# The last gate's sums: from DVE in the attention heads to POOL and ScalarE in the first units of the token mixing

## The chip, the cores and the metric

The kernel runs on one core of a Trainium2 chip. The metric is the device time of one execution in microseconds (us), as a median of several runs. Five engines work side by side, each in the order of its own instruction list: PE (TensorE, matrix products; its weight loads are listed as PEld), DVE (VectorE), ACT (ScalarE), POOL (GpSimd) and SP (SyncE), which here issues all transfers (DMA). Engines wait for each other by semaphores.

## The reference, cut to what matters

One block on x of 2048 tokens by 1024 channels: a conditioned attention with a memory, then an MLP over the token axis. Six vectors of 1024 come from a conditioning vector `c`; the last one, `gb`, scales the MLP's output.

```python
mod = (_silu(c) @ w_mod).reshape(c.shape[0], 6, 1, -1)
sa, ca, ga, sb, cb, gb = (mod[:, 0], mod[:, 1], mod[:, 2], mod[:, 3], mod[:, 4], mod[:, 5])
h = _layernorm(x, axis=-1) * (1 + ca) + sa
x = x + ga * _A_ref(h, A_wq, A_wk, A_wv, A_wo, A_beta)
h = _layernorm(x, axis=-1) * (1 + cb) + sb
x = x + gb * _B_ref(h, B_w1, B_b1, B_w2, B_b2)
...
# in _B_ref
u = jnp.einsum("bsd,sf->bdf", h, w1) + b1
u = _gelu(u)
y = jnp.einsum("bdf,fs->bds", u, w2) + b2
```

## The kernel before

The work has four stages.

*Start (0 to about 100 us).* `c` passes through SiLU into `sc` (a column) and `scb` (the same 1024 numbers on every partition). The first two vectors, `sa` and `ca`, are made here.

*Heads (to about 990 us).* 32 iterations of four heads each: `project` (matmuls of L194 and L202), `maxima`, `scores`, `values`. A hand-written plan (`plan`, `later`, `todo`) puts side work at given heads n. The remaining four vectors of `mod` are side work: at head 40 + 2j, `mod_fetch(j)` loads 128 rows of `w_mod` transposed (512 KB, tile `rawm`), and two heads later `mod_late(j)` (L531) multiplies them with `scb` on DVE and adds up each row into column j of `mcol`. Eight columns make one vector, so j = 24 to 31 is the gate `gb`. After j = 7 and after j = 31 `mod_rows` transposes the finished columns on PE and writes them to DRAM (`modd`); `spread(dst, i)` (L567) loads row i of `modd` onto all partitions.

*Output projection (to about 1212 us)* of 16 token tiles, with the second layernorm. It ends in the inputs of the mixing.

*Mixing (to the end).* Both products of the MLP use seven products in place of eight (a Strassen scheme, `NPR = 7`). The first half has 28 units: `ph` 0 and 1, `g` 0 to 13. A unit is one `mix`: seven products q of 12 matmuls each. For each unit `prepare` loads 1 MB of weights (`wr`, two buffers), makes the seven operands' sums on DVE, and splits each operand (tile `sp`, seven buffers) into a high part by ACT (L121) and a low part by DVE (L124). A product lands in a PSUM bank and is evicted to `cc`: by ACT (L831) if it is the first to reach its quarter in `ph` 0, otherwise by DVE as an addition (L833). Products 0, 2, 4 and 6 go on in the same bank, so each must be evicted before the next begins. `pcd[g]` keeps the result of `ph` 0. Beside units 1 to 9 of `ph` 0 run the `bias_rows` (L875 to L880): for each of 16 token tiles a row block `x1d` is loaded, `gb * b2` is added by DVE (L879), and the result goes to `x1e`. They need `gb`, which is loaded at the end of unit 1. In `ph` 1 `gb` also multiplies each unit's output (L962). The second half (w2) has 40 units and begins at about 1765 us.

The order of instructions on each engine is fixed when the kernel is compiled: a scheduler takes the program's order as priority and simulates the engines. Tiles with the same tag share their buffers in turn, and a load into a buffer waits for its last reader.

Of the kernel before, what the change touches and what calls it, by code (L numbers as in the profile page):

```python
# [7 lines left out]
F32 = mybir.dt.float32  # L8
# [3 lines left out]
AF = mybir.ActivationFunctionType  # L12
ALU = mybir.AluOpType
# [4 lines left out]
S, D, H, DH, F = 2048, 1024, 32, 32, 3584  # L18
P = 128
# [3 lines left out]
NT = S // P  # L23
# [15 lines left out]
WO0 = 65  # L39
# [6 lines left out]
def attention_and_mlp(ctx, tc, x, wq, wkv, wo, beta, w1, b1, w2, b2, c, wm_a, wm_b, out):  # L46
    nc = tc.nc
    V, A, G, T, SY = nc.vector, nc.scalar, nc.gpsimd, nc.tensor, nc.sync

    dram = ctx.enter_context(tc.tile_pool(name="dram", bufs=1, space=DRAM))  # L50
    oT = dram.tile([NG, P, S], F32, name="oT")
    modd = dram.tile([4, D], F32, name="modd")
    x1d = dram.tile([NT, P, D], F32, name="x1d")
    x1e = dram.tile([NT, P, D], F32, name="x1e")
    hcd = dram.tile([8, P, 7, 512], F32, name="hcd")
# [10 lines left out]
    a = par.__enter__()  # L66
    scb, gaw = (a.tile([P, D], F32, name=n) for n in ("scb", "gaw"))
# [8 lines left out]
    def bank(tag, bufs, name):  # L76
        return psum.tile([P, 512], F32, tag=tag, bufs=bufs, name=name)
# [94 lines left out]
    def keep_w(g):  # L172
        for kind, n in (("v", 4), ("q", 2)):
            for i in range(n):
                SY.dma_start(wsp[g, i if kind == "v" else 4 + i], W[0, g][kind, i].bitcast(F32))
# [126 lines left out]
    b = late.__enter__()  # L302
# [220 lines left out]
    mcol = const.tile([P, 4 * NK], F32, name="mcol")  # L523

    def mod_fetch(j):
        r = a.tile([P, D], F32, tag="raw", bufs=3, name=f"rawm{j}")
        SY.dma_start(r, wm_b[P * j:P * j + P])
        return r

    def mod_late(j, r):  # L530
        V.scalar_tensor_tensor(r, r, 1.0, scb, op0=ALU.mult, op1=ALU.mult, accum_out=mcol[:, j:j + 1])  # L531
        if j == 7:
            mod_rows(0, 8)
        if j == 31:
            V.tensor_scalar_add(mcol[:, 16:24], mcol[:, 16:24], 1.0)
            mod_rows(8, 32)

    def mod_rows(lo, hi):
        n = hi - lo
        ps = bank("ms", 1, f"mlt{lo}")  # L540
        T.transpose(ps[0:n, 0:128], mcol[:, lo:hi], ident)
        row = pj.tile([n, P], F32, tag="tmp", bufs=2, name=f"mrow{lo}")
        A.copy(row, ps[0:n, 0:128])
        SY.dma_start(modd.rearrange("a (b n) -> (a b) n", n=P)[lo:hi], row)
# [3 lines left out]
    def plan(n, f, engines=""):  # L548
        todo.setdefault(n, []).append((f, engines))
# [16 lines left out]
    def spread(dst, i):  # L566
        SY.dma_start(dst, bass.AP(tensor=modd.tensor, offset=modd.offset + D * i, ap=[[0, P], [1, D]]))  # L567
# [19 lines left out]
    def wo_fetch(i):  # L587
        nh, c2 = i // 4, 2 * (i % 4)
        r = a.tile([P, 2, 512], F32, tag="raw", bufs=3, name=f"wor{i}")
        SY.dma_start(r, wo[P * c2:P * c2 + 2 * P, 512 * nh:512 * nh + 512].rearrange("(c p) n -> p c n", p=P))  # L590
        return r

    def wo_split(i, r):

        nh, c2 = i // 4, 2 * (i % 4)
        hi = a.tile([P, 2, 512], F32, tag="raw", bufs=3, name=f"woh{i}")
        for j in range(2):
            G.tensor_tensor(r[:, j], r[:, j], gaw[:, 512 * nh:512 * nh + 512], op=ALU.mult)
            A.copy(hi[:, j].bitcast(F32R), r[:, j])
            V.tensor_tensor(r[:, j].bitcast(F32R), r[:, j], hi[:, j], op=ALU.subtract)  # L600
        for part, t in enumerate((hi, r)):
            SY.dma_start(wos[c2:c2 + 2, nh, :, part].rearrange("c p n -> p c n"), t)

    def later(n, fetch, m, f, engines):

        got = []
        plan(n, lambda: got.append(fetch()))
        plan(m, lambda: f(got[0]), engines)
# [4 lines left out]
    for g in range(2, NG):  # L613
        n = 8 * g - 13
# [2 lines left out]
            later(n + n0, lambda g=g, kind=kind, part=part: fetch_part(g, kind, part),  # L617
                  n + n1, lambda r, g=g, kind=kind, part=part: split_part(g, kind, part, r), "A")
        plan(n + 4, lambda g=g: keep_w(g))
    for j in range(32):  # L620
        n = ML0 + MLS * j
        later(n, lambda j=j: mod_fetch(j), n + 2, lambda r, j=j: mod_late(j, r), "V")
    plan(WO0 - 3, lambda: spread(gaw, 0))
    for i in range(8):
        n = WO0 + WOS * i
        later(n, lambda i=i: wo_fetch(i), n + 2, lambda r, i=i: wo_split(i, r), "G")

    for n in range(-LEADS, 4 * NI + VL):
# [15 lines left out]
        if 4 * NI - 5 <= m < 4 * NI + 3:  # L644
            i = m - 4 * NI + 5
# [46 lines left out]
    def b_tile(pool, nk, q, name):  # L692
        return pool.tile([P, nk, 2, 512], F32R, tag=f"B{q}", bufs=1, name=f"{name}_{q}")
# [144 lines left out]
    def load_b(stg, src, nk, dsts, q, name, bufs=2):  # L838

        r = stg.tile([P, nk, 512], F32, tag="bst", bufs=bufs, name=f"bst{name}_{q}")  # L840
        SY.dma_start(r, src[:, :, SLOT[q]].rearrange("k p n -> p k n"))
        for k in range(nk):
            split(dsts[k], r[:, k], A, V)
# [5 lines left out]
    def y_tile(name):  # L849
        return yb.tile([P, 4, 512], F32, tag="ac", bufs=4, name=name)  # L850
# [31 lines left out]
    def cc_tile(ph, g):  # L882
        cc = cp.tile([P, 4, 512], F32, tag="cc", bufs=3, name=f"cc{ph}_{g}")
        if ph:
            SY.dma_start(cc, pcd[g])
        return cc

    def w2_unit(ph, g):
        k0, nk = sum(KP[:ph]), KP[ph]
        return prepare(w2[g, :, 512 * k0:512 * (k0 + nk)].rearrange("p (b n) -> p b n", b=4), nk)  # L890

    acc = {}

    def start_acc(g, pool):
# [7 lines left out]
    row = 0  # L902
    for u, (ph, g) in enumerate(units):
        cc = cc_next
        if g == 0:
            nxt = {}
        last = u + 1 == len(units)
        if last:
            unit_2 = w2_unit(0, 0)

        def after(q):
            if u < 2:
                n = 7 * u + q
                if n in (2, 5, 8):
                    rest[(2, 5, 8).index(n)]()
            if q == 3 and not last:
                cc_next_[0] = cc_tile(*units[u + 1])
            if g < NG1 - 1:
                return
            if ph == 0:  # L920
                if q % 2 == 0 and q < 6:
                    return
                for r in (q - 1, q) if q < 6 else (q,):
                    if r % 2 == 0:
                        b2_ = y_tile(f"bB1_{r}")
                    a_, b_ = b_tile(b3, 3, r, "bA1"), b2_[:, 2 * (r % 2):2 * (r % 2) + 2].bitcast(F32R)
                    load_b(tp, hcd[4:8], 4, [a_[:, 0], a_[:, 1], a_[:, 2], b_], r, "h4")
                    nxt[r] = (a_, b_)
            else:
                if q in (1, 3, 5, 6):  # L930
                    start_acc({1: 0, 3: 1, 5: 2, 6: 3}[q], yb)
                for i in {3: (0,), 4: (1,), 5: (2, 3), 6: (4, 5, 6)}.get(q, ()):
                    unit_2[1].pop(0)()
                nxt[q] = next_b(tp, 0, q)

        cc_next_ = [None]
        mix(unit, 4, lambda q, k: bA[q][:, k] if k < 3 else bB[q], cc, ph == 0, after)
        cc_next = cc_next_[0]
        if not last:
            unit = prepare(w1[units[u + 1]], 4)  # L940
        if u == 1:
            cw_pool.__exit__(None, None, None)
            tp_pool = tc.tile_pool(name="g1t", bufs=1, reuse_waits="tile")
            tp = tp_pool.__enter__()
            gb = tp.tile([P, D], F32, name="gb")
            spread(gb, 3)
            b1s = tp.tile([P, FT], F32, name="b1s")
            SY.dma_start(b1s, b1)
            b2s = tp.tile([P, NT], F32, name="b2s")
            SY.dma_start(b2s, b2)  # L950
        if ph == 0:
            SY.dma_start(pcd[g], cc)
            if g == NG1 - 1:
                bA, bB = [nxt[q][0] for q in range(NPR)], [nxt[q][1] for q in range(NPR)]
            for tt in range(row, min(row + (0, 1, 2)[min(g, 2)], NT)):
                bias_rows(tt)
                row = tt + 1
            continue
        for m in range(2):
            c2 = cc[:, 2 * m:2 * m + 2].rearrange("p a n -> p (a n)")  # L960
            A.activation(c2, c2, AF.Gelu_apprx_tanh, bias=b1s[:, g + NG1 * m:g + NG1 * m + 1])
            V.tensor_tensor(c2, c2, gb, op=ALU.mult)  # L962
        t = tp.tile([P, 3, 512], F32, tag="tu", bufs=1, name=f"tu{g}")
        t_combos(G, cc[:, 0], cc[:, 1], cc[:, 2], cc[:, 3], t)
        SY.dma_start(ucd[g, :, 0:4], cc)
        SY.dma_start(ucd[g, :, 4:7], t)
# [3 lines left out]
    yac, tp = (ctx.enter_context(tc.tile_pool(name=n, bufs=1, reuse_waits="tile")) for n in ("yac", "g2t"))  # L970
# [59 lines left out]
```

## Time and profile before

| | us |
|---|---|
| median of 3 runs | 2292.65 (2292.54 to 2294.87) |
| the profiled execution | 2297.73 |
| its span, first to last instruction | 2296.0 |
| PE busy | 2223.2 (97%) |
| DVE busy | 1673.7 (73%) |
| ACT busy | 1148.6 (50%) |
| POOL busy | 734.0 (32%) |

All times within the kernel come from the one profiled execution and count from its first instruction. Busy time is the union of an engine's instructions; matmuls overlap each other, so a busy PE is not necessarily PE at its peak. "Idle before" in a row of the timeline is the time that the engine stood still ahead of that instruction, and the name behind the arrow is what ended it. L12 is line 12 of the kernel.

### The profile page before, as it was taken

How to read it: one execution, taken by the hardware profiler on the slowest of the kernel's cores; microseconds unless marked ns; L12 is line 12 of the kernel's file. 1: busy time of each engine (PE TensorE's matmuls, PEld its weight loads, DVE VectorE, ACT ScalarE, POOL GpSimd, SP SyncE). 2: the span in 40 equal slices, each digit the busy share in tenths (PEclk: the TensorE clock that was granted, in tenths of full speed). 3: DMA queues.
4: the chain of work that ended last, by engine and by line, in shares of the span. 5: the costliest groups of instructions: out<-in, count | busy, mean ns of one | idle time of the engine just before them, and what ended most of it. 6: DMA issues, size and time to landing. Idle time of an engine off the chain costs nothing.

```text
span 2296.0 us, 38430 instructions
## 1 busy us (share of the span) xinstructions
PE 2223.2 (97%) x13802; PEld 1907.4 (83%) x13802; DVE 1673.7 (73%) x3798; ACT 1148.6 (50%) x2090; POOL 734.0 (32%) x843
## 2 busy tenths in 40 slices
PE   7999999998999999998999999999999999999999
PEld 6888898888988889977887888888887888888887
DVE  6686676765777777665867655688889787878787
ACT  6477677665656666655545333443334242424232
POOL 5165665564766766653001000023333000000000
PEclk9999999999999999997999999999999999999999
DMA  6656565687566566662465754556557441414133
GB/s 257 202 167 187 156 194 151 180 284 215 166 188 203 170 191 186 198 231 92 148 222 208 262 214 164 200 222 239 205 206 260 177 151 56 152 56 142 55 120 147
DMA packets 172595, 414.67 MB, mean 181 GB/s; under 512 B 17237, under 2 KB 71541, under 8 KB 163445
## 3 DMA queue, kind: packets, MB, share of 16 engines
q1 hardware_dynamic: 172404, 412.22, 54.9%
q8 instruction: 110, 1.80, 0.3%
q14 instruction: 81, 0.66, 0.1%
HBM read 236.23 MB, written 125.06 MB: 157 GB/s over the span
## 4 chain that ended last, share of the span: by engine, by line
PE 77%; DMA 8%; DVE 6%; ACT 4%; POOL 3%; issue 2%; SPq 0%; DVEq 0%; ACTq 0%; POOLq 0%
PE mx L826 40%; PE nps L194 12%; PE qps L202 7%; PE po L729 6%; PE pv L502 3%; DMA xb<-x1d 2%; DMA x1e<-xb 2%; POOL ph L488 1%; PE sx L438 1%; PE a L473 1%; PE sz L438 1%; DMA sk<-nt 1%; PE rd L410 1%; ACT ph L486 1%; PE a L476 1%
## 5 line engine op out<-in xcount | busy, mean ns | idle before, releaser
L826 PE MATMUL mx<-bU,sp 128*128 128x512 f32 x2352 | 536.1, 390 | 2.7 <-DVE sp L124 1.1
L826 PEld LDWEIGHTS mx<-bU,sp 128*128 128x128 f32 x2352 | 440.8, 188 | 97.5 <-DVE sp L124 1.9
L194 PE MATMUL nps<-wv,h 128*128 128x256 f32 x3072 | 435.3, 283 | 4.6 <-POOL h L124 4.3
L121 ACT CAST sp<-wr 128x384 fp32r<-128x384 f32 (+2 forms) x408 | 216.7, 545 | 443.9 <-PE mx L826 362.9
L826 PE MATMUL mx<-bA,sp 128*128 128x512 f32 x1764 | 433.3, 391 | 5.6 <-DVE cc L833 2.4
L488 POOL TENSOR_TENSOR ph<-p,ph 128x640 f16<-128x640 f32 x256 | 376.9, 1493 | 151.8 <-ACT ph L486 151.5
L194 PEld LDWEIGHTS nps<-wv,h 128*128 128x128 f32 x3072 | 402.7, 189 | 12.0 <-POOL h L124 5.7
L826 PEld LDWEIGHTS mx<-bA,sp 128*128 128x128 f32 x1764 | 331.8, 188 | 77.5 <-DVE cc L833 3.2
L124 DVE TENSOR_TENSOR sp<-wr,sp 128x384 fp32r<-128x384 f32 (+2 forms) x408 | 257.0, 642 | 30.8 <-ACT sp L121 30.4
L833 DVE TENSOR_TENSOR ac<-mx,ac 128x512 f32<-128x512 f32 x280 | 189.4, 685 | 90.2 <-PE mx L826 89.5
L202 PE MATMUL qps<-h,wq 128*128 128x512 f32 x768 | 199.5, 406 | 2.3 <-DVE pv L505 1.1
L729 PE MATMUL po<-wo,ots 128*128 128x512 f32 x768 | 180.9, 395 | 5.0 <-DVE x L732 2.8
L486 ACT CAST ph<-p 128x1280 f16<-128x1280 f32 x128 | 161.1, 1259 | 44.3 <-POOL p L484 43.5
L729 PEld LDWEIGHTS po<-wo,ots 128*128 128x128 f32 x768 | 145.2, 190 | 35.4 <-ACT ots L121 2.3
L439 DVE CUSTOM_DVE_ANT_0 sx<-sx,mask 128x128 f32<-128x128 f32 (+1 forms) x256 | 110.0, 430 | 87.9 <-PE sx L438 86.6
L202 PEld LDWEIGHTS qps<-h,wq 128*128 128x128 f32 x768 | 144.0, 194 | 31.6 <-issue 2.9
L484 POOL TENSOR_SCALAR_AFFINE_SELECT p<-p 128x256 f32<-128x256 f32 x256 | 121.3, 482 | 132.9 <-ACT p L477 70.2
L826 PE MATMUL mx<-bB,sp 128*128 128x512 f32 x588 | 163.8, 390 | 0.0
L502 PE MATMUL pv<-vp,ph 128*128 128x97 bf16 (+1 forms) x2560 | 148.2, 205 | 4.5 <-POOL ph L488 1.6
L502 PEld LDWEIGHTS <-ph 128*128 128x128 f16 x2560 | 118.5, 100 | 30.4 <-issue 12.3
L826 PEld LDWEIGHTS mx<-bB,sp 128*128 128x128 f32 x588 | 110.3, 188 | 23.3 <-DVE bB L124 0.4
L687 POOL TENSOR_TENSOR tu<-cc 128x512 f32<-128x512 f32 x14 | 20.0, 1426 | 339.8 <-DVE cc L962 284.0
(198 smaller groups left out, 3286.7 us busy)
## 6 DMA issues: line engine op xcount, KB each, us to landing
sk<-sg SPq DMA_DIRECT2D x384, 128.0 KB
wr<-in_w_dram SPq DMA_DIRECT2D x28, 1024.0 KB
wr<-in_w_dram SPq DMA_DIRECT2D x32, 768.0 KB
bstu<-ucd SPq DMA_DIRECT2D x28, 768.0 KB
wsp<-wv SPq DMA_DIRECT2D x32, 512.0 KB
rawm<-in_wm_b_dram SPq DMA_DIRECT2D x32, 512.0 KB
wv<-wsp SPq DMA_DIRECT2D x32, 512.0 KB
pcd<-cc SPq DMA_DIRECT2D x14, 1024.0 KB
```

Of the source, the lines that this page charges most:

```text
L121: A.copy(hi, src)
L124: lo_eng.tensor_tensor(lo, src, hi.bitcast(F32), op=ALU.subtract)
L194: T.matmul(ps[:, aa], h[:, j, 128 * tt:128 * tt + 128], wt[:, i, o:o + 256], start=(n == 0), stop=(n >= 6 * NK - 2), skip_group_check=True)
L202: T.matmul(ps, wt[:, i, o:o + 128], h[:, j], start=(k + n == 0), stop=(3 * k + n == 3 * NK - 1))
L439: marks[4 * t + h - LEADS, "V"] = V.tensor_tensor_reduce(o, o, mask[:, 384 - 128 * i:], 1.0, -3.0e38, op0=ALU.add, op1=ALU.max, accum_out= ...
L484: G.affine_select(w, w, pattern=[[0, 2], [1, 128]], compare_op=ALU.is_ge, fill=0.0, base=0, channel_multiplier=-1)
L486: marks[n, "A"] = A.copy(ph[:, 0], p32)
L488: marks[n, "G"] = G.tensor_tensor(ph[:, 1, c], p32[:, c], ph[:, 0, c], op=ALU.subtract)
L502: T.matmul(pv[:, i, 0:w], ph[:, part, o:o + 128], d["vp"][:, j, h, 0:w], start=(n == 0), stop=(n == 19), skip_group_check=True)
L729: T.matmul(ps, os_[:, i, P * ct:P * ct + P], wop[ct, nh][:, j], start=(n == 0), stop=(n == 3 * NK - 1))
L826: T.matmul(ps, ops[q][:, i, P * k:P * k + P], b[:, j], start=(m == 0 and first), stop=(m == 3 * nk - 1), skip_group_check=True)
L833: V.tensor_tensor(d, ps, d, op=ALU.add)
```

## The change

Columns 24 to 31 of `mcol` are no longer made in the heads. There, the sums end with j = 23, and 16 rows are transposed in place of 24. One row of `scb` is kept in DRAM (`scd`). At the end of units 1 to 4 of the mixing (program order), `gate_sums` loads two blocks of `w_mod` at once (1 MB, tile `mw`, one buffer), multiplies each with `scl` (`scb` loaded back onto all partitions) on POOL and adds up its rows on ACT. After the last one, the eight columns are written to `modd` by one transfer, element by element, and `gb` is spread from there. The bias rows begin at unit 5 and run two per unit up to unit 12. `scl` uses the buffer (`tu`) that the bias rows use afterwards.

```diff
+    scd = dram.tile([1, D], F32, name="scd")
...
-        if j == 31:
+        if j == 23:
             V.tensor_scalar_add(mcol[:, 16:24], mcol[:, 16:24], 1.0)
-            mod_rows(8, 32)
+            mod_rows(8, 24)
...
-    for j in range(32):
+    for j in range(24):
         n = ML0 + MLS * j
         later(n, lambda j=j: mod_fetch(j), n + 2, lambda r, j=j: mod_late(j, r), "V")
     plan(WO0 - 3, lambda: spread(gaw, 0))
+    plan(WO0, lambda: SY.dma_start(scd, scb[0:1]))
...
+    def gate_sums(j):
+
+        if j == 24:
+            scl.append(tp.tile([P, 3, 512], F32, tag="tu", bufs=1, name="scl").rearrange("p a n -> p (a n)")[:, 0:D])
+            SY.dma_start(scl[0], bass.AP(tensor=scd.tensor, offset=scd.offset, ap=[[0, P], [1, D]]))
+        r = tp.tile([P, 2, D], F32, tag="mw", bufs=1, name=f"mw{j}")
+        SY.dma_start(r, wm_b[P * j:P * j + 2 * P].rearrange("(a p) n -> p a n", p=P))
+        for i in range(2):
+            G.tensor_tensor(r[:, i], r[:, i], scl[0], op=ALU.mult)
+            A.activation(r[:, i], r[:, i], AF.Copy, accum_out=mcol[:, j + i:j + i + 1])
+        if j == 30:
+            SY.dma_start(modd[3].rearrange("(b n) -> n b", n=P), mcol[:, 24:32])
+            spread(gb, 3)
+
+    scl = []
...
             gb = tp.tile([P, D], F32, name="gb")
-            spread(gb, 3)
...
-            for tt in range(row, min(row + (0, 1, 2)[min(g, 2)], NT)):
+            if 1 <= g < 5:
+                gate_sums(22 + 2 * g)
+            for tt in range(row, min(row + 2 * (g >= 5), NT)):
                 bias_rows(tt)
                 row = tt + 1
```

## The prediction

> **What bounds the kernel now.** The page comes first: which engine is full, and what the chain that ended last is made of.
>
> ```profile
> span 2296.0 us, 38430 instructions
> PE 2223.2 (97%) x13802; PEld 1907.4 (83%) x13802; DVE 1673.7 (73%) x3798; ACT 1148.6 (50%) x2090; POOL 734.0 (32%) x843
> PE 77%; DMA 8%; DVE 6%; ACT 4%; POOL 3%; issue 2%; SPq 0%; DVEq 0%; ACTq 0%; POOLq 0%
> ```
>
> TensorE (PE) is busy 97% of the span and holds 77% of the chain, so work on another engine is worth only what it makes PE wait. I therefore read the two places that the change touches stage by stage, in the view of busy time by windows: the heads in which the last eight sums now lie, and the first half of the mixing, where they go.
>
> ```profile
> 780.00:840.00 60.00, 57.91 (x515) 52.55 (x514) 41.09 (x131) 37.01 (x68) 36.88 (x47) 1.00 0.60 170
> 840.00:900.00 60.00, 59.76 (x524) 54.39 (x521) 47.00 (x143) 39.58 (x71) 42.30 (x51) 1.00 0.66 199
> 900.00:960.00 60.00, 60.00 (x548) 55.44 (x547) 39.38 (x121) 38.71 (x69) 40.00 (x51) 1.00 0.56 148
> 1210.00:1470.00 260.00, 254.45 (x1106) 207.77 (x1105) 160.61 (x243) 96.98 (x176) 6.07 (x4) 0.99 0.55 203
> ```
>
> The columns are the stretch, its length, then busy time (and count) of PE, PE's weight loads, DVE, ACT and POOL. In the heads PE is busy 117.67 of 120 us between 780 and 900; DVE has a quarter of its time free. In the mixing POOL is empty (6 of 260 us), ACT is 37% busy, PE idles 5.6 us in all. The view of waits over 1210 to 1470 us says on whom PE waited where the profile names it:
>
> ```profile
> PE mx L826 <- DVE cc L833: 2.4, 2, 1.6
> PE mx L826 <- ACT sp L121: 2.0, 1, 2.0
> PE mx L826 <- ACT cc L831: 1.1, 3, 0.7
> ```
>
> So both stages are PE's, the second with a few microseconds of evictions (`cc`, L831 on ACT, L833 on DVE) that came late.
>
> **What leaves the heads.** Eight sums (columns 24 to 31) go, each one DVE product with its accumulator read, and a load of 512 KB.
>
> ```profile
> L531 DVE SCALAR_TENSOR_TENSOR rawm<-rawm,scb x9: 1208/1222/2222, 769.7 to 885.7; 128x1024 f32<-128x1024 f32 x9
> L531 DVE DVE_READ_ACCUMULATOR rawm<-rawm,scb x9: 71/77/84, 770.9 to 886.9; 128x1 f32 x9
> ```
>
> That is 8 x (1.22 + 0.08) = 10.4 us of DVE between about 780 and 887 us, and 4 MB of loads on SP's queue. DVE is not the bound there, so most of it buys nothing. The gain is bounded below by about -1 us (the compiled order of all engines shifts from head 88 on, with no direction to it) and above by 5.2: the 60 us without sums hold 548 matmuls against 519.5 on average in the two before, 5% of 120 us is 6.2 us, less one for the different mix of matmuls at the end. PE's idle time in those 120 us, 2.33 us, is the nearer row, because it is the time that a shorter DVE queue could give back. I take -1.5.
>
> The rest of the stage's edit is free: the row of `scb` written to DRAM is one 4 KB transfer, which the compiled order puts among the first loads of the start, behind them on SP, and the 16 remaining rows of the gate are transposed 116 us earlier (769.7 for 885.7) than 24 were, long before L723 reads them.
>
> **What leaves the first mixing units.** The 16 bias rows (L879) sat in units 1 to 9; now they sit in units 5 to 12. The first of them cost PE a visible stop, by the timeline (start, duration, what; in brackets the idle time before and what ended it):
>
> ```profile
> 1251.45 1.28 DVE L879 SCALAR_TENSOR_TENSOR xb<-gb,b2s,xb 128x1024 f32<-128x1024 f32 x1 [2.79 <-DMA xb<-x1d]
> 1252.65 0.68 DVE L833 TENSOR_TENSOR cc<-mx,cc 128x512 f32<-128x512 f32 x1
> 1253.39 2.83 PE L826 MATMUL mx<-bA,sp 128*128 128x512 f32 x11 [1.60 <-DVE cc L833]
> 1338.93 1.43 PE L826 MATMUL mx<-bA,sp 128*128 128x512 f32 x5 [0.78 <-DVE cc L833]
> ```
>
> DVE stood 2.79 us for the row's transfer, then made it, then evicted; PE waited 1.60 us for that eviction. It falls in the stretch where the units are still being filled, and no bias row is left there: -1.6. The 0.78 us at 1338.93 is an ordinary collision of a later bias row; 16 rows remain, so it stays: 0.
>
> **What comes in.** In each of units 1 to 4: a load of 1 MB, two POOL products of 128x1024, two ACT row sums of 128x1024, serial, because the tile `mw` has one buffer. The nearest rows for the products (512 wide) and for the sums:
>
> ```profile
> L598 POOL TENSOR_TENSOR wor<-wor,gaw x16: 1268/1295/2332, 622.2 to 929.2; 128x512 f32<-128x512 f32 x16
> L286 ACT ACTIVATE wm<-wm x4: 1053/1057/1064, 33.9 to 45.8; 128x1024 f32<-128x1024 f32 x4
> L286 ACT ACTIVATION_READ_ACCUMULATOR wm<-wm x4: 183/186/187, 34.9 to 46.8; 128x1 f32 x4
> ```
>
> A product is 2 x 1.295 = 2.6 us, a row sum 1.06 + 0.19 = 1.25. The 10 us of ACT fit into its idle time; what matters is that ACT runs in order. A row sum that waits for POOL holds the casts and evictions behind it. The nearest 1 MB loads are those of `wr`:
>
> ```profile
> 1300.20 0.39 SPq L786 DMA_DIRECT2D wr<-in_w_dram  x1
> 1306.35 0.69 DVE L796 TENSOR_TENSOR s<-wr 128x512 f32<-128x512 f32 x1 [0.37 <-DMA wr<-in_w_dram]
> 1315.91 0.33 SPq L786 DMA_DIRECT2D wr<-in_w_dram  x1
> 1324.27 0.69 DVE L796 TENSOR_TENSOR s<-wr 128x512 f32<-128x512 f32 x1 [0.56 <-DMA wr<-in_w_dram]
> ```
>
> They landed after 6.15 and 8.36 us; I take 7, and write L for it. One round is then 0.3 (issue) + 7 + 2 x 2.6 + 1.25 = 13.75 us, and the next load waits on SP for the round's last sum. The first round starts where the loads of `gb` and of the first bias row stood, at about 1246:
>
> ```profile
> 1245.45 0.43 SPq L878 DMA_DIRECT2D xb<-x1d  x1
> 1258.57 0.62 ACT L121 CAST sp<-wr 128x512 fp32r<-128x512 f32 x1 [8.55 <-PE mx L826]
> 1260.59 2.20 PE L826 MATMUL mx<-bA,sp 128*128 128x512 f32 x9
> 1291.50 0.59 ACT L831 COPY cc<-mx 128x512 f32<-128x512 f32 x1 [3.40 <-PE mx L826]
> 1295.83 2.65 PE L826 MATMUL mx<-bA,sp 128*128 128x512 f32 x11
> ```
>
> The order of the compiled kernels shows PE's order in these units almost unchanged, so the rows of before tell when each eviction and cast is needed. Round 1: its sums stand in ACT's queue just ahead of the cast at 1258.57 (operand 5 of unit 2), in the 8.55 us that ACT idled. They end at 1253 + 5.2 + 1.25 = 1259.45; the cast then ends at 1260.1 and DVE's low part 0.7 later, at 1260.8. PE wants that operand at 1260.59, or 1.6 earlier now that its stop is gone: 1259.0. The first matmuls wait 1.1 us, the third, which needs the low part, another 0.4 to 1.0: 2.1 in all, +2.1 (0 if the load lands 2 us earlier, 5 if 3 later). PE then stands 0.5 us behind its old place.
>
> Round 2 ends at 1273.2 and delays nothing that PE needs at once. Round 3's first sum ends at 1273.2 + 0.3 + 7 + 2.6 + 1.25 = 1284.35 and the eviction behind it just in time. Round 4's first sum stands ahead of the eviction at 1291.50 (product 6 of unit 2), which frees the bank of unit 4's product 0. Round 3 ends at 1286.95, this sum at 1286.95 + 11.15 = 1298.1, the eviction at 1298.7. PE wants the bank after two of the 11 matmuls at 1295.83 (0.23 us each), at 1296.28, now 1296.8: +1.9. In terms of L the eviction ends at 1277.7 + 3L, so PE's stop is 0 at L = 6.4 and 6 at 8.36, the bounds of the range here.
>
> The products also take DVE's way. The last products that POOL made in this stage show it:
>
> ```profile
> 1234.03 1.30 POOL L688 TENSOR_TENSOR tc<-h,tc 128x512 f32<-128x512 f32 x1 [6.63 <-ACT h L748]
> 1234.43 1.45 DVE L124 TENSOR_TENSOR sp<-wr,sp 128x512 fp32r<-128x512 f32 x1 [1.82 <-ACT sp L121]
> 1236.99 1.75 POOL L690 TENSOR_TENSOR tc<-h,tc 128x512 f32<-128x512 f32 x1
> 1237.50 1.78 DVE L124 TENSOR_TENSOR bB<-bsth,bB 128x512 fp32r<-128x512 f32 x1
> 1253.25 0.68 DVE L124 TENSOR_TENSOR sp<-s,sp 128x512 fp32r<-128x512 f32 x1
> ```
>
> A DVE subtraction that takes 0.68 us elsewhere (the last row) took 1.45 and 1.78 beside POOL, which itself took 1.75 instead of 1.30. With products twice as long a low part can come 2.6 us late, a product 0.45. DVE is idle for 99 of the stage's 260 us, 7 in a unit of 19, so I price this at +1 in all (0 to 9: eight times 2.6 less the 1.5 us of margin that the cast of round 1 had).
>
> [...]
>
> **The gate itself.** It is ready only after round 4: last sum 2.6 us later, 1300.7, then a write of 1024 single elements to DRAM, then the broadcast `gb`, and the first bias row on DVE waits for it, ahead of unit 4's evictions.
>
> ```profile
> 1303.49 1.28 DVE L879 SCALAR_TENSOR_TENSOR xb<-gb,b2s,xb 128x1024 f32<-128x1024 f32 x1 [0.86 <-DMA xb<-x1d]
> 1316.91 4.24 PE L826 MATMUL mx<-bA,sp 128*128 128x512 f32 x18
> ```
>
> At about 1303 DVE comes to that row. From it to the eviction of unit 4's product 4 lie two bias rows and eight ordinary operations, 2 x 1.28 + 8 x 0.69 = 8.1 us; PE needs it nine matmuls into the 18 at 1316.91, at 1318.95. So `gb` may land as late as 1310.9, or 1313.3 with PE's 2.4 us of delay. The scatter has no row; between 2 us and the 8.36 of the slowest large load, I take 3, since it is only 4 KB. The broadcast: the bias row's load issued at 1245.45 was there 6.0 us later. 1300.7 + 0.6 + 3 + 6 = 1310.3: hidden, 0, with 3 us to spare; 2 us of stop if the scatter takes 8.36. The load of `wr` for unit 6 stands behind `gb` on SP and is 4 us late (1300.20 before); it lands at 1311, for a DVE step that comes then. 0.
>
> [...]
>
> **The sum.** -1.5 - 1.6 + 2.1 + 1.9 + 1 = +1.9 us. The profiled execution took 2297.73 us (2296.0 of span and 1.73 around), 5.08 above the median of 2292.65. 2299.6 on its scale is 2294.6 on that of the median. A measurement here tells about 0.2%, 4.6 us, from no change.
>
> **The rivals.** Slower, the chain of rounds: at L = 8.36 PE's stop is 6.0 in place of 1.9, so +6.0 in all, 2298.7. It decides from L = 7.9, where it alone makes 4.6. For it: the slower `wr` row; against: units 1 to 4 lose the bias rows' 1 MB each. Chance 0.22. [...] Chance 0.13.
>
> Faster, all is hidden: L below 6 and the heads give 5.2, with round 1 at 1: -5.2 - 1.6 + 1 = -5.8, 2286.9. For it the 548 matmuls after the last sum, against it the 2.33 us of idle PE. Chance 0.13. That the sums leave the heads is certain from the compiled order, that PE notices is not.
>
> My forecast has 0.52. Its own range is 2289 to 2297: heads at -5.2 and no stop in round 4 at the one end, heads at +1 at the other. To hold eight in ten the range takes in the chain and half of the lock: 2287 to 2303. Below -4.6 us 0.14, within 0.51, above 0.35.
>
> **What would show it.** Right: PE's stop at 1253.39 gone, a wait of PE for an ACT cast or low part near 1260 and for an ACT eviction near 1297, ACT's row sums waiting for POOL for some us in rounds 1 and 4, no PE wait behind the first bias row, 117 to 118.5 us of busy PE in the heads' same stretch and its end 0 to 3 us earlier. Wrong: the heads end over 4 us earlier or later, loads of `mw` under 5 or over 8 us, or DVE standing for `gb` past 1313.

## The result, and the profile after

The changed kernel takes 2306.77 us (median of 6 runs, 2303.36 to 2309.64) against 2292.6 us for the kernel before on the same chip: ratio 1.0061, 95% interval 1.0050 to 1.0072. It is 14 us slower. The profiled execution has a span of 2307.9 us, 11.9 more than that of before.

The page first: the same PE instructions, and little more work on any engine.

```profile
span 2307.9 us, 38418 instructions
PE 2228.7 (97%) x13802; PEld 1913.5 (83%) x13802; DVE 1676.9 (73%) x3782; ACT 1156.9 (50%) x2106; POOL 753.5 (33%) x851
PE 78%; DMA 6%; DVE 6%; ACT 4%; POOL 3%; issue 2%; SPq 0%; DVEq 0%; ACTq 0%; POOLq 0%
```

Shares do not show where 12 us went. The windows used for before do (the stretch, its length, then busy time and count of PE, its weight loads, DVE, ACT, POOL; granted clock, DMA share, GB/s):

```profile
780.00:840.00 60.00, 59.55 (x522) 54.43 (x522) 38.42 (x125) 38.64 (x70) 38.21 (x50) 1.00 0.54 151
840.00:900.00 60.00, 59.55 (x522) 54.03 (x521) 38.61 (x129) 38.87 (x69) 38.42 (x52) 1.00 0.55 160
1210.00:1470.00 260.00, 246.41 (x1051) 199.70 (x1050) 166.50 (x231) 100.30 (x181) 27.65 (x12) 0.97 0.62 216
1360.00:1370.00 10.00, 10.00 (x46) 8.29 (x45) 6.31 (x10) 3.19 (x6) 0.00 (x0) 1.00 0.39 130
```

In the 260 us of the mixing PE did 1051 matmuls where it did 1106. An undisturbed 10 us hold 46 (last row), so 55 matmuls are 12.0 us: the whole difference between the two profiled executions lies here. Of it, 8.0 us are PE standing still (246.41 busy for 254.45). The rest, 4 us, is a lower granted clock, 0.57 over 7 us where the rows below show it, which comes after the stops. The timeline names the stops (start, duration, what; in brackets the idle time before and what ended it):

```profile
1212.78 4.88 PE L828 MATMUL mx<-bA,sp 128*128 128x512 f32 x20 [1.73 <-ACT sp L122]
1260.22 2.34 PE L828 MATMUL mx<-bA,sp 128*128 128x512 f32 x9 [1.91 <-ACT cc L833]
1320.19 2.74 PE L828 MATMUL mx<-bA,sp 128*128 128x512 f32 x7 [2.91 <-DVE sp L125]
1324.75 3.71 PE L828 MATMUL mx<-bA,sp 128*128 128x512 f32 x9 [1.82 <-DVE cc L835]
1348.97 4.21 PE L828 MATMUL mx<-bA,sp 128*128 128x512 f32 x9 [3.48 <-DVE cc L835]
```

The same view by windows, for the 7 us behind the stops:

```profile
1320.00:1327.00 7.00, 4.99 (x12) 3.52 (x13) 5.11 (x8) 2.63 (x5) 0.00 (x0) 0.57 0.39 150
1349.00:1356.00 7.00, 7.00 (x18) 5.50 (x19) 2.41 (x4) 1.11 (x2) 0.00 (x0) 0.57 0.85 314
```

Near 1320 and from 1349 on the granted clock is 0.57 over 7 us. PE needed 4.99 and 7.00 us there for 12 and 18 matmuls, which take 2.6 and 3.9 us at 46 in 10 us: 5.5 us lost. Before, one such stretch stood at the start of the stage, where 20 matmuls took 6.52 us for 4.88 now (1.6 us). The difference of 3.9 us is the rest that was sought; over the 260 us the clock is 0.99 before and 0.97 now.

All three late stops name DVE. The timeline of DVE itself, with SP's beside it:

```profile
1294.53 0.37 SPq L905 DMA_DIRECT2D modd<-mcol  x1
1310.40 0.32 SPq L568 DMA_DIRECT2D gb<-modd  x1
1315.65 1.28 DVE L881 SCALAR_TENSOR_TENSOR xb<-gb,b2s,xb 128x1024 f32<-128x1024 f32 x1 [13.08 <-issue]
1330.05 1.29 DVE L881 SCALAR_TENSOR_TENSOR xb<-gb,b2s,xb 128x1024 f32<-128x1024 f32 x1 [4.16 <-DMA xb<-x1d]
1339.73 1.28 DVE L881 SCALAR_TENSOR_TENSOR xb<-gb,b2s,xb 128x1024 f32<-128x1024 f32 x1 [5.74 <-DMA xb<-x1d]
```

The write of the eight columns into `modd`, 1024 single elements, 4 KB, was issued at 1294.53. The load of `gb`, which waits for its end, went out at 1310.40, 15.9 us later. DVE stood 13.08 us at the first bias row, with the evictions and low parts of units 4 and 5 behind it. And the write did more than come late. In the windows of 4 us, the last two columns are the DMA share and the GB/s; this view puts a packet wholly into the window in which it began, which is how a share can pass 1:

```profile
1294.00:1298.00 4.00, 4.00 (x19) 3.34 (x18) 2.37 (x4) 2.12 (x5) 0.00 (x0) 1.00 0.88 279
1298.00:1302.00 4.00, 4.00 (x20) 3.30 (x19) 1.48 (x4) 2.21 (x4) 0.00 (x0) 1.00 1.82 191
1302.00:1306.00 4.00, 4.00 (x19) 3.31 (x18) 0.57 (x1) 0.64 (x2) 0.00 (x0) 1.00 0.51 20
```

In the third window hardly a packet began (20 GB/s), since those of the second still ran. The trace's single packets show why. The write's own packets did not start at its issue: 990 packets of under 512 bytes stand between 1298.9 and 1300, behind a bias row and a store of `cc` (1.5 MB together) that SP had issued 0.8 to 1.2 us ahead of it. The 8 KB packets that began in the next 8 us, those of the next store of `cc`, took 1.96 us each (median; up to 6.3), against 0.31 ahead of the write, with all 16 DMA engines taken up (16 to 18 packets under way at every half microsecond from 1300 to 1307.5). So of the 15.9 us some 4.4 are a wait for the transfers ahead, and 11.5 pass from the write's first packets to its end.

### The profile page after: what moved, and what is told of

Its sections match the earlier page's. It is cut to its first block, busy times and chain, and to the rows that moved or that the text cites. A ratio compares the mean times of both kernels' runs of the same rounds, so it can differ in the third digit from the quotient of the medians.

```text
span 2307.9 us, 38418 instructions
## 1 busy us (share of the span) xinstructions
PE 2228.7 (97%) x13802; PEld 1913.5 (83%) x13802; DVE 1676.9 (73%) x3782; ACT 1156.9 (50%) x2106; POOL 753.5 (33%) x851
## 4 chain that ended last, share of the span: by engine, by line
PE 78%; DMA 6%; DVE 6%; ACT 4%; POOL 3%; issue 2%; SPq 0%; DVEq 0%; ACTq 0%; POOLq 0%
PE mx L828 40%; PE nps L195 12%; PE qps L203 8%; PE po L731 6%; PE pv L503 3%; POOL ph L489 1%; PE sx L439 1%; PE a L474 1%; PE sz L439 1%; PE rd L411 1%; PE a L477 1%; DMA sk<-nt 1%; POOL mw L902 1%; PE a L481 1%; DMA x<-in_x_dram 1%
## 5 line engine op out<-in xcount | busy, mean ns | idle before, releaser
L125 DVE TENSOR_TENSOR sp<-wr,sp 128x384 fp32r<-128x384 f32 (+2 forms) x408 | 265.6, 662 | 30.6 <-ACT sp L122 30.4
L835 DVE TENSOR_TENSOR cc<-mx,cc 128x512 f32<-128x512 f32 x140 | 94.5, 684 | 37.7 <-PE mx L828 36.7
```

The costliest lines, as they stand in the source:

```text
L125: lo_eng.tensor_tensor(lo, src, hi.bitcast(F32), op=ALU.subtract)
L835: V.tensor_tensor(d, ps, d, op=ALU.add)
```

## The experiments

Each kernel was run with five rounds (one with three) beside the kernel before. Single runs of one kernel scatter by up to 8 us either way, so the intervals matter. Two theories stood at first: the element-wise write, or something else in the change (the heads, the moved bias rows, POOL's products). Line numbers in the rows are those of each kernel.

**The write, in runs of 32 bytes.** The order of all instructions stays that of the changed kernel. The transposition is left out, so the gate's entries stand in another order.

```diff
-            SY.dma_start(modd[3].rearrange("(b n) -> n b", n=P), mcol[:, 24:32])
+            SY.dma_start(modd[3].rearrange("(n b) -> n b", b=8), mcol[:, 24:32])
```

> The changed kernel with one transfer altered: the eight columns go to DRAM as 128 runs of 32 bytes in place of 1024 single elements (left out: the transposition, so the gate's entries stand in another order). Every engine's compiled order is that of the changed kernel. Theory 1, the element-wise write alone is the cause: SP's wait for it falls from 12.1 us to under 3, DVE's stand at the first bias row from 13.1 us to under 3, PE's stops of 2.91 and 1.82 us and the halved clock behind them go, 9 to 13 us less than the changed kernel, 2293 to 2298 us. Rival, the serial rounds of products and row sums, or the bias rows' later place: these are untouched, so 2303 us or more.

Measured: 2296.83 us, ratio 1.0015 (1.0000 to 1.0030). The same 4 KB in 128 runs took 5.65 us from issue to the load of `gb`, and the late stops are gone. Here too the write waited for its turn: only 16 of the 176 packets of under 512 bytes in this stretch began before 1291.5, 4.3 us after the issue, so from its packets to its end it took 1.3 us. SP's and DVE's timelines:

```profile
1287.19 1.51 SPq L905 DMA_DIRECT2D modd<-mcol  x1
1292.84 0.32 SPq L568 DMA_DIRECT2D gb<-modd  x1
1297.99 1.28 DVE L881 SCALAR_TENSOR_TENSOR xb<-gb,b2s,xb 128x1024 f32<-128x1024 f32 x1 [3.27 <-issue]
```

**The write, transposed on PE first.** One PE transpose, one ACT copy, then eight runs of 512 bytes. (`scl[1]` is an identity matrix and `scl[2]` room for the copy, both in unused parts of the buffer of `scl`.)

```diff
-            SY.dma_start(modd[3].rearrange("(b n) -> n b", n=P), mcol[:, 24:32])
+            ps = bank("ms", 1, "mlt24")
+            T.transpose(ps[0:8, 0:128], mcol[:, 24:32], scl[1])
+            A.copy(scl[2], ps[0:8, 0:128])
+            SY.dma_start(modd[3].rearrange("(b n) -> b n", n=P), scl[2])
```

> The changed kernel, but the eight columns are turned by PE (one transpose through an unused PSUM bank, a copy by ACT) and written as 8 rows of 512 bytes. Theory 1: as with the runs of 32 bytes, 2293 to 2298 us, some 10 us under the changed kernel, the transpose itself about 0.3 us of PE. Rival (the rounds or the rows): 2303 us or more.

Measured: 2293.63 us, ratio 0.9996 (0.9984 to 1.0008). All the rest of the change is in this kernel, the later place of the bias rows too, and costs nothing that can be told. Its timelines: the write took 1.2 us, DVE stood 0.29.

```profile
1301.71 0.29 SPq L912 DMA_DIRECT2D modd<-scl  x1
1302.93 0.34 SPq L568 DMA_DIRECT2D gb<-modd  x1
1308.15 1.28 DVE L881 SCALAR_TENSOR_TENSOR xb<-gb,b2s,xb 128x1024 f32<-128x1024 f32 x1 [0.29 <-DMA xb<-x1d]
```

**The heads alone**: the eight sums left out, the mixing as before, the gate taken from another row.

```diff
+            spread(gb, 2)
...
-            if 1 <= g < 5:
-                gate_sums(22 + 2 * g)
-            for tt in range(row, min(row + 2 * (g >= 5), NT)):
+            for tt in range(row, min(row + (0, 1, 2)[min(g, 2)], NT)):
```

> The heads' half of the change alone: the eight sums leave the heads and are not made anywhere (left out: the gate, which is read from another row), the bias rows and the mixing are as before. Theory 1: the heads end level with before, because what the changed kernel is ahead at head 104 (4.9 us) is lost again while the last weights are loaded; time within 3 us of before. Rival, the heads' gain is real and is only eaten later: 4 to 6 us faster than before.

Measured: 2294.11 us, ratio 1.0003 (0.9993 to 1.0014). Ten microseconds of DVE work removed from the heads are worth nothing.

**The mixing half alone**: the sums stay in the heads too.

```diff
-        if j == 23:
+        if j == 31:
...
-    for j in range(24):
+    for j in range(32):
```

> The mixing half of the change alone: the eight sums stay in the heads too (and are made a second time in the mixing, as in the changed kernel). If the heads neither gain nor lose by giving up the sums, 2305 to 2309 us like the changed kernel; if they give 5 us, 2310 to 2314 us.

Measured: 2307.16 us, ratio 1.0063 (1.0047 to 1.0079), like the whole change. The two halves add up: 0 and 14 us.

**The bias rows alone**: the kernel before, its 16 rows begun at unit 5 in program order.

```diff
-            for tt in range(row, min(row + (0, 1, 2)[min(g, 2)], NT)):
+            for tt in range(row, min(row + 2 * (g >= 5), NT)):
```

> The kernel before with nothing changed but the place of the bias rows: units 5 to 12 in place of 1 to 9, the gate still made in the heads. Theory 1: DVE has no gate to wait for, so within 2 us of before, perhaps 1.6 faster by the stop of PE that the first row made. Rival, the later place is what costs: 5 to 12 us slower than before, with PE stops near 1349 us.

Measured: 2291.33 us, ratio 0.9992 (0.9980 to 1.0004): -1.8 us, with 0 and the -1.6 of the prediction both inside. But the edit hardly moved the rows: the scheduler filled them in as before, PE's and ACT's orders are those of the kernel before, and DVE's and SP's differ in a few places. DVE's timeline has the first row at its old place, now without a wait:

```profile
1250.23 1.28 DVE L879 SCALAR_TENSOR_TENSOR xb<-gb,b2s,xb 128x1024 f32<-128x1024 f32 x1
```

So this run doesn't test the later place of the rows; the kernel with the transposed write does (first row at 1308.15).

So it is the write. Open was how it costs: by the gate's lateness, because DVE stands for it, or by holding up all transfers.

**DVE held elsewhere.** The bias rows are queued on DVE behind unit 4's last eviction, so that nothing of unit 4 stands behind the gate.

```diff
+                evict[0] = V.tensor_tensor(d, ps, d, op=ALU.add)
...
             if 1 <= g < 5:
                 gate_sums(22 + 2 * g)
+                held[0] = evict[0].ins
...
+                with tc.issue_after(held[0]):
-                bias_rows(tt)
+                    bias_rows(tt)
```

> The changed kernel with the element-wise write as it was, but the bias rows held on DVE behind the last eviction of unit 4, eight DVE operations later. Theory 1 (the late gate costs because DVE stands for it ahead of unit 4's evictions): the gate lands at about 1316 as before, DVE comes to the row only at about 1323 and does not stand for it, PE's stops of 2.9, 1.8 and 3.5 us and the two stretches at half clock go, 2294 to 2299 us. Theory 2 (the write costs by holding up the other transfers, the weights of unit 6 above all, whoever waits for the gate): the stops stay, 2303 to 2308 us.

Measured: 2304.98 us (five executions), ratio 1.0055 (1.0039 to 1.0072). The loss stays. A sixth execution, the profiled one, took 4402.93 us, for a cause that is not known, with 674 ns for a matmul of the mixing instead of 389; so the kernel was run again for its trace.

> The kernel with the bias rows held behind unit 4's last eviction once more, for its trace (the profiled execution of the first run was of another kind, 4402.93 us), 2303 to 2308 us. If the gate's lateness was the whole cause, DVE now has no stand of over 4 us ahead of unit 4's evictions and PE none of its stops, and the time stays unexplained; if the transfers held up by the write are the cause, DVE stands for the weights of unit 6 (issued behind the gate's load on SP) or for the bias rows, and PE stops as before, at other places.

Measured: 2305.57 us, ratio 1.0054 (1.0036 to 1.0071). DVE does not stand for the gate any more, but for the weights of unit 6, nearly as long (SP's and DVE's timelines):

```profile
1290.16 1.29 SPq L905 DMA_DIRECT2D modd<-mcol  x1
1305.57 0.42 SPq L788 DMA_DIRECT2D wr<-in_w_dram  x1
1312.25 0.69 DVE L798 TENSOR_TENSOR s<-wr 128x512 f32<-128x512 f32 x1 [12.39 <-DMA wr<-in_w_dram]
```

They were issued late, at 1305.57, because `gb` ahead of them on SP waits for the write. This could be SP's queue alone, so:

**The broadcast issued by POOL**, which is idle then; nothing on SP waits for the write.

```diff
-            spread(gb, 3)
+            G.dma_start(gb, bass.AP(tensor=modd.tensor, offset=modd.offset + D * 3, ap=[[0, P], [1, D]]))
```

> The changed kernel, the element-wise write as it was, but the broadcast of the gate issued by POOL, which is idle then, so that nothing stands behind it on SP: the weights of unit 6 are issued 12 us earlier. If the standing queue of SP is what costs, 2293 to 2299 us; if the write itself holds up the transfers, or the late gate holds DVE, 2303 to 2308 us and PE's stops as in the changed kernel.

Measured: 2306.07 us, ratio 1.0052 (1.0036 to 1.0069). It was not SP's standing, by the same two timelines:

```profile
1298.08 0.37 SPq L788 DMA_DIRECT2D wr<-in_w_dram  x1
1316.65 0.69 DVE L798 TENSOR_TENSOR s<-wr 128x512 f32<-128x512 f32 x1 [12.01 <-DMA wr<-in_w_dram]
```

The weights left at 1298.08, 7.5 us earlier than in the kernel above, and landed at 1316.65, 18.6 us after their issue, where this size took 6.2 and 8.4 before. They were still on the same DMA queue as the write (q1 of the profile, which has all that SP issues); whether transfers on another queue would have passed it was not tried.

**The write alone, for nobody.** The kernel before, every instruction of PE, DVE, ACT and POOL in its place, with one more transfer: 1024 elements of `cc` to a spare row that no one reads.

```diff
-            SY.dma_start(pcd[g], cc)
+            SY.dma_start(pcd[g], cc); g == 3 and SY.dma_start(spare[0].rearrange("(b n) -> n b", n=P), cc[:, 0, 0:8])
```

> The kernel before, with one more transfer: at the end of unit 3 of the mixing 1024 single elements of cc are written to a row of DRAM that nobody reads; order of PE, DVE, ACT and POOL as before. Theory 1 (lateness of the gate): the loads of the next bias rows behind it come some us later, DVE stands for one of them, 2292 to 2297 us. Theory 2 (held-up transfers): DVE stands 8 us or more for the rows behind it and PE stops for 5 us or more, 2299 to 2305 us.

Measured: 2301.70 us, ratio 1.0039 (1.0025 to 1.0052). Nothing waits for this write (between 1275 and 1345 us no instruction of ACT or DVE stood for it), and it costs about 9 us by the ratio. The timelines of SP and DVE:

```profile
1279.48 0.37 SPq L952 DMA_DIRECT2D spare<-cc  x1
1281.85 0.32 SPq L880 DMA_DIRECT2D x1e<-xb  x1
1291.63 0.32 SPq L878 DMA_DIRECT2D xb<-x1d  x1
1295.67 1.28 DVE L879 SCALAR_TENSOR_TENSOR xb<-gb,b2s,xb 128x1024 f32<-128x1024 f32 x1 [10.12 <-DMA xb<-x1d]
```

The bias row's store behind it took 9.8 us (the next row's load, which waits for it, leaves at 1291.63), so DVE stood 10.12 us. Of the trace's packets, those of 4 KB that began between 1283 and 1290 took 1.2 us (median) for 0.16 ahead of the write. PE's stop of 3.87 us came only at 1338: one row's load waits for the row before it, so a late row makes late rows.

**Its control**, the same additional transfer in 128 runs of 32 bytes; the compiled orders are equal.

```diff
-... spare[0].rearrange("(b n) -> n b", n=P), cc[:, 0, 0:8])
+... spare[0].rearrange("(n b) -> n b", b=8), cc[:, 0, 0:8])
```

> The kernel before with the same additional transfer of 4 KB out of unit 3 that nobody waits for, now as 128 runs of 32 bytes in place of 1024 single elements; all else as in that run. If the single elements are what holds up the transfers behind them, DVE's stand for the next bias row falls from 10 us to under 6 and the time to 2291 to 2295 us; if any additional transfer at this place costs (its issue on SP, its reading of cc), 2299 to 2304 us as with the elements.

Measured: 2293.71 us, ratio 1.0011 (1.0002 to 1.0020). The store behind it is through in 2.6 us, and its 4 KB packets take 0.16 us. The timelines:

```profile
1282.19 0.32 SPq L952 DMA_DIRECT2D spare<-cc  x1
1285.22 0.32 SPq L880 DMA_DIRECT2D x1e<-xb  x1
1287.84 0.32 SPq L878 DMA_DIRECT2D xb<-x1d  x1
1291.48 1.28 DVE L879 SCALAR_TENSOR_TENSOR xb<-gb,b2s,xb 128x1024 f32<-128x1024 f32 x1 [2.56 <-DMA xb<-x1d]
```

**A late gate without single elements.** Runs of 32 bytes (again without the transposition), then four copies from row to row of DRAM.

```diff
-            SY.dma_start(modd[3].rearrange("(b n) -> n b", n=P), mcol[:, 24:32])
+            SY.dma_start(hop[0].rearrange("(n b) -> n b", b=8), mcol[:, 24:32]); [SY.dma_start(hop[i + 1], hop[i]) for i in range(4)]; SY.dma_start(modd[3], hop[4])
```

> The gate written in runs of 32 bytes, as in the run that cost nothing, then copied four times from row to row of DRAM and once into its place, so that it comes late without single elements; the first bias row stands on DVE behind unit 4's last eviction, and the weights of unit 6 ahead of the copies on SP. If a late gate with a late train of bias rows is enough, 2303 to 2308 us, with PE's stops of 2 to 4 us some 10 and 30 us after it; if it takes the held-up transfers, 2293 to 2298 us.

Measured: 2298.02 us, ratio 1.0024 (1.0010 to 1.0038), single runs from 2293.8 to 2307.0: at the upper edge of what the second theory allows. The gate came even later than in the changed kernel, and PE has no stop between 1267 and 1377; then it stood 1.79 and 2.02 us, at 1377 and 1418, for evictions of DVE. DVE's timeline:

```profile
1317.44 1.29 DVE L881 SCALAR_TENSOR_TENSOR xb<-gb,b2s,xb 128x1024 f32<-128x1024 f32 x1 [5.61 <-issue]
```

The weights stood ahead of the copies and landed within 5.4 us, so DVE had work until 1311.8. DVE's order here is near that of the two kernels at 2305 to 2306 us above, not that of the changed kernel. What the same lateness costs in the changed kernel's own order is therefore not separated.

**Half the elements.** 512 of them right after the second round, where nobody waits, the other four columns as runs of 16 bytes.

```diff
-            SY.dma_start(modd[3].rearrange("(b n) -> n b", n=P), mcol[:, 24:32])
+            SY.dma_start(modd[3, 0:512].rearrange("(b n) -> n b", n=P), mcol[:, 24:28])
+            SY.dma_start(modd[3, 512:1024].rearrange("(n b) -> n b", b=4), mcol[:, 28:32])
```

> The changed kernel with the write cut in two: 512 elements as soon as the first four columns are there (after round 2, where nobody waits for them), the other four columns after round 4 as 128 runs of 16 bytes (so half of the gate is permuted). Theory 1 (lateness): the second write takes 5 to 6 us as that in runs of 32 bytes did, DVE stands 0 to 4 us, 2294 to 2299 us. Theory 2 (held-up transfers): half of the elements hold up the transfers half as long, in round 3, about half of the 10 us between the two forms, 2300 to 2303 us.

Measured: 2300.77 us, ratio 1.0037 (1.0025 to 1.0050), half-way, as the held-up transfers would have it. But the runs of 16 bytes took 7.2 us and DVE stood 7.24 us for `gb`, so a part of it is that second write. It does not decide by itself.

**Two buffers for the bias rows**, so that a row's load need not wait for the row before.

```diff
+        if tt % 2:
+            r = tp.tile([P, 2, D], F32, tag="mw", bufs=1, name=f"xb{tt}")[:, 0]
+        else:
```

> The changed kernel, the bias rows alternating between two buffers (tu and mw), so that a row's load need not wait for the row before it to be written out. If the loss is made by the train of rows behind a late first one (each row 8 to 9 us after the one before, DVE standing for each), the stops 30 us after the write and about half of the loss go, 2297 to 2302 us; if by the first stand alone, 2303 to 2308 us.

Measured: 2303.02 us, ratio 1.0043 (1.0028 to 1.0058). The last stop is gone, but the one before it grew to 5.44 us, since two rows now stand ahead of the evictions. PE's timeline:

```profile
1323.79 4.20 PE L828 MATMUL mx<-bA,sp 128*128 128x512 f32 x9 [5.44 <-DVE cc L835]
```

It is 4 us faster than the changed kernel, with intervals that overlap.

**The mended write with the two buffers**, as a candidate for the best version (the two edits above together).

> The changed kernel with the eight columns transposed on PE and written as eight runs of 512 bytes (the run that came out even with the kernel before), and the bias rows alternating between two buffers. If the train of bias rows still costs PE something in that version, 2288 to 2291 us, below both kernels; if what is left is round 1's stop of PE for ACT, 2292 to 2295 us.

Measured: 2295.76 us, ratio 1.0021 (1.0010 to 1.0032). That is above both ranges: no gain; no version beat the kernel before by more than the measurement can tell.

One number separates the kernels: the longest time that DVE stood for a transfer between 1270 and 1330 us, in each kernel's profiled execution. (Later rows make DVE stand for up to 6.6 us in kernels that lose nothing.)

| kernel | longest stand, us | for | ratio |
|---|---|---|---|
| before | 4.7 | bias row | 1 |
| bias rows alone | 4.8 | bias row | 0.9992 |
| transposed write | 2.4 | bias row | 0.9996 |
| heads alone | 4.4 | bias row | 1.0003 |
| spare write, runs of 32 B | 4.6 | bias row | 1.0011 |
| runs of 32 B | 4.1 | bias row | 1.0015 |
| transposed write, two buffers | 2.4 | bias row | 1.0021 |
| late gate by copies | 5.6 | gate | 1.0024 |
| half the elements | 7.2 | gate | 1.0037 |
| spare write, elements | 10.1 | bias row | 1.0039 |
| elements, two buffers | 10.6 | gate | 1.0043 |
| elements, broadcast by POOL | 12.0 | weights | 1.0052 |
| elements, rows held | 12.4 | weights | 1.0054 |
| the change | 13.1 | gate | 1.0061 |
| mixing half alone | 11.2 | gate | 1.0063 |

With a full write of single elements DVE stands 10 to 13 us, whatever it is that it waits for; without any it stands under 6, and the ratio stays at 1.0024 or below. Within each of the two groups the number does not order the ratios well.

## Why the prediction was wrong

The step that failed is the term "The scatter has no row; between 2 us and the 8.36 of the slowest large load, I take 3, since it is only 4 KB". It measured 15.9 us, outside both bounds. Two things went wrong in it. The price was chosen by bytes, while it went by the pieces: of 4 KB each, 1024 single elements took 11.5 us from their first packets to their end, 128 runs 1.3 us, and 8 runs were through 1.2 us after their issue. And the term left out the wait for the 1.5 MB ahead, 4.4 us. The rest of the chain can be followed: with 15.9 for 3, the write issued at 1294.5 instead of about 1301 and a broadcast of 5.25 us, the gate is there at 1315.65, 4.75 past the 1310.9 that the prediction allowed. PE's two stops at 1320 and 1325 are 2.91 + 1.82 = 4.73. That the two agree so closely is partly luck, since the first stop ended with a low part of DVE and not with the eviction that the prediction looked at. So "hidden, 0" fell with the scatter. Of the signs of error that were named, DVE standing for `gb` past 1313 came, and a load of `mw` of under 5 us too (below).

Two costs behind it were in no step. The write held up the transfers behind it (the spare write's 9 us), which made the bound "2 us of stop" too small even in kind: in the kernel with POOL's broadcast it is the weights that come late. And with the stops came a lower granted clock (0.50 for 6.83 us, twice), 5.5 us of matmul time. The pieces can be counted in the traces: between the write's issue and the gate's load 1084 packets were under 512 bytes, against 176 between the same two issues with runs of 32 bytes. The "1024 single elements" of the forecast should have led to a rival with a price per piece; no rival of the prediction was a late gate.

The other terms, one by one:

- The heads, -1.5: worth 0 (the heads alone, +0.7 us with an interval of -1.6 to +3.2). PE's idle time in the 120 us fell from 2.33 to 0.90, as thought, but it was lost again right behind: between 930 and 1020 us PE stood still for 4.95 us, against 1.45 before, most of it (3.33 and 1.46) at the start of the output projection, where it waits for DVE. The first PE stop of the mixing ended at 1212.78, and in the timeline of before at 1212.57. One pair of executions can't tell 1.5 us, though: in the kernel with the runs of 32 bytes, whose order is the same, it ended at 1204.03.

```profile
1212.57 6.52 PE L826 MATMUL mx<-bA,sp 128*128 128x512 f32 x20 [2.00 <-ACT sp L121]
```

- The first bias row's stop, -1.6: gone as forecast.
- Round 1, +2.1: right in size, 1.91 us at 1260.22, though it came from an eviction of ACT behind the row sums and the cast, and not from the cast itself. ACT's timeline:

```profile
1259.60 0.57 ACT L833 COPY cc<-mx 128x512 f32<-128x512 f32 x1
```

- Round 4, +1.9: none. The first load took 7.5 us and the last 4.9 (issues at 1245.2 and 1283.2 in the groups of the changed kernel, here with the accumulator reads, to the first and last starts of POOL below), where 7 was assumed. The last sum was read at 1294.3, and the rival of the chain of rounds fell with that. Its formula was off, too: 1277.7 + 3L counts the loads of rounds 2 to 4, but the end of round 1 that it starts from holds a fourth L.

```profile
L900 SPq DMA_DIRECT2D mw<-in_wm_b_dram x4: 373/382/433, 1245.2 to 1283.2; - x4
L903 ACT ACTIVATION_READ_ACCUMULATOR mw<-mw x8: 182/184/188, 1256.2 to 1294.3; 128x1 f32 x8
```

- POOL against DVE, +1: the collisions are there (beside the products seven DVE operations took 1.15 to 2.88 us in place of 0.69), but no PE stop names them. The forecast's range also takes in half of "the lock", in which each of the eight products would stop a part that PE needs (+9 in place of +1); no run shows such a term. In its place, PE's only stop of more than 0.3 us between 1250 and 1300 us, 1.91 us, ended with an eviction of ACT. The products and a DVE operation of 0.69 us that met one, by the timelines of POOL and DVE:

```profile
1252.71 5.29 POOL L902 TENSOR_TENSOR mw<-mw,scl 128x1024 f32<-128x1024 f32 x2 [14.35 <-DMA mw<-in_wm_b_dram]
1255.78 2.77 DVE L802 TENSOR_TENSOR wr<-wr 128x512 f32<-128x512 f32 x1
...
1288.12 5.20 POOL L902 TENSOR_TENSOR mw<-mw,scl 128x1024 f32<-128x1024 f32 x2 [6.11 <-DMA mw<-in_wm_b_dram]
```

Without the scatter the total came out: the kernel with the transposed write took 2293.63 us, and 2294.6 had been forecast. That is in part luck, because three of the five terms (-1.5, +1.9, +1) came to about 0, and they nearly cancel (+1.4). What stays open is how the 14 us divide between the gate's lateness and the held-up transfers in the changed kernel's own order, why single elements slow the packets behind them, and why two buffers helped there (if they did: the intervals overlap) but not with the mended write.

## What to carry to other kernels

Price a transfer by its pieces as well as its bytes (4 KB took 11.5 us from its first packets in 1024 pieces, 1.3 in 128), and by what stands ahead of it in the queue (4.4 us here); where no row of the trace has that shape, carry the price per piece through as a rival of its own. A write of single elements was no private matter of its reader here (the one that nobody read cost 9 us): look at what else is in flight then, above all at what an in-order engine will wait for next. Here the eight columns could be turned on PE first: one transpose and eight long runs cost nothing that could be told (ratio 0.9996).

## What the runs showed of the hardware

- 4 KB written as 1024 elements took 15.9 us, 4.4 of them behind 1.5 MB of other transfers; for 8 us the 8 KB packets beside it took 1.96 us (median) instead of 0.31. A 1 MB load issued 3.5 us after it (in the kernel with POOL's broadcast) landed after 18.6 us instead of 6 to 8. Having POOL issue the load that waits for the write did not help those behind it on SP's queue.
- The granted clock was 0.50 for 6.83 us from 1320.94, 0.75 us behind the end of the stop of 2.91 us, and again from 1348.25, 2.76 us into the stop of 3.48. In the 3.41 us (half that length) ahead of 1348.25 PE had been busy for 0.65 us. In the kernel with the rows held it was 0.50 for as long from 1315.18, behind a stop of 1.83 us; a second stop, of 1.07 us, fell within that stretch. There PE had been busy for 1.58 of the 3.41 us ahead. After the changed kernel's stop of 1.91 us, which ended at 1260.22, the clock stayed at 1.00 (windows of 10 us from 1250 to 1270). So a stop's length alone does not decide it, and what does is not shown (PE's ends are modelled, so its true gaps may be longer than shown). By windows, the changed kernel:

```profile
1344.84:1348.25 3.41, 0.65 (x3) 0.19 (x2) 1.61 (x3) 2.50 (x5) 0.00 (x0) 1.00 0.39 143
1348.25:1355.08 6.83, 6.11 (x14) 4.79 (x15) 3.16 (x6) 0.59 (x2) 0.00 (x0) 0.50 0.78 284
```

The kernel with the rows held, its timeline of PE and its windows:

```profile
1314.33 2.65 PE L828 MATMUL mx<-bA,sp 128*128 128x512 f32 x7 [1.83 <-DVE sp L125]
1318.05 4.16 PE L828 MATMUL mx<-bA,sp 128*128 128x512 f32 x9 [1.07 <-DVE cc L835]
```

```profile
1311.77:1315.18 3.41, 1.58 (x8) 0.98 (x7) 2.86 (x5) 0.10 (x1) 0.00 (x0) 1.00 0.00 0
1315.18:1322.01 6.83, 5.76 (x14) 4.02 (x13) 4.01 (x6) 2.53 (x5) 0.00 (x0) 0.50 0.42 149
```
